# Three token blocks instead of two take turns over the first MLP's weights, with partial sums added up in DRAM

## The chip, the core and the metric

The kernel runs on one core of a Trainium2 chip. The metric is the device time of one execution in microseconds (us). The engines are PE (matrix products), DVE and ACT (vector and activation work, both read PSUM), POOL (vector work without PSUM), and SP, which in this kernel only issues DMAs.

## The reference, cut to what matters

```
X = fft(fft(x, axis=1), axis=2).real          # x: 2 x 3008 x 256
x = X.reshape(6016, 256)
h = x @ w_in;  g = relu(h) ** 2;  x = g @ w_out            # first MLP, 256 -> 2048 -> 256
h = x @ w2_in; g = h * sigmoid(1.702 * h); out = g @ w2_out # second MLP, the same sizes
```

## The kernel before

**Tiling.** The 6016 tokens (two batches) are eight blocks of some 752 columns, four blocks for each batch. A block's columns lie in two halves of 376 to 378 that share one product by symmetry. The kernel has an opening (loads of x, three folds of x and the transform along the features for batch 0, the first weights), then the first MLP for all blocks, and behind it the second MLP, which starts some 520 us into the span.

**Steps of the first MLP.** The hidden width of 2048 is cut into 16 chunks `f`, so there are 8 x 16 = 128 steps. Step i does in this order: `front1` (6 matmuls of chunk f into a psum tile of pool `psa`, 2 buffers), `back` of the step that lies four earlier (`LAG = 4`, 12 matmuls into the two accumulators of its block, pool `psb`, 2 buffers), then on DVE the row `p` (L685) and the two rows `h` (L687, L688), on ACT relu, square and the rounded part `gh` (L694, L695, L697; the steps in `SV` do relu and square on DVE, L692), and on POOL the remainder `gl` (L75; the steps in `VSTEPS` on DVE). A step is named below by its number, and it begins with its `p` on DVE.

**Weights.** They come as 64-bit words. `widen` makes of one group (4 chunks of f; there are 4 groups in, 4 groups out) an exact pair of a rounded part and a remainder: rows L158, L159, L166, L168 on DVE (L157, L163 on ACT; L165 on DVE in one case), L188 on POOL and L189 on DVE for the input weights, L191 on ACT, and the remainder on POOL (on DVE for in 1 and out 3). Group g of the input weights is needed when a step reaches f = 4g, group g of the output weights four steps later.

**Turns.** Because a group takes long to widen, the first two blocks take turns over what is there, and a block that leaves its turn unfinished writes its two accumulators to DRAM (`store`); `fetch_partial` reads them back and the block's last `store` adds them on DVE (L571):

```
turns = [(0, 0, 0, 4), (0, 1, 0, 8), (0, 0, 4, 16), (0, 1, 8, 16)]   # (mlp, block, from f, to f)
turns += [(0, j, 0, 16) for j in range(2, 8)]
```

**Background.** All other work (widening, the transform of further blocks, the folds of batch 1, the second MLP's weights) runs between the steps. `PLAN` gives for each job the step at which it begins, how many of its pieces are emitted for each step, and the step before which it must be through. `even_k` makes blocks 0 and 1 of a batch, `odd_k` blocks 2 and 3 (two sums of 16 matmuls of 376 columns each, L328, their evacuation L386 and L387, and `split_eo`, L336 and L75). The framework orders each engine's queue itself from the emitted program, and only from step 18 on (`THROTTLE`) background work is held behind the step's own rows. Every queue runs in order. `o` (the copy of an accumulator that is stored) and `h` share a ring of four buffers, so an `h` can wait until the DMA of an `o` has landed.

Of the kernel before, what the change touches and what calls it, by code (L numbers as in the profile page):

```python
# [16 lines left out]
P = 128  # L17
# [15 lines left out]
PLAN = {  # L33
# [29 lines left out]
def spectral_two_mlps_kernel(  # L63
# [33 lines left out]
    cp = tc.alloc_tile_pool(name="cp", bufs=3, side="right", reuse_waits="tile")  # L97
    xp = tc.alloc_tile_pool(name="xp", bufs=3, side="left")

# [3 lines left out]
    def load_x(q):  # L103
        b, c = divmod(q, NC)
        xq[q] = xp.tile([P, 2, 8, P], F32, tag="xt", name="xt")
        src = x8[b, c].rearrange("p (r a t) -> p r a t", r=2, a=8)
        for a in XPARTS[q]:
            nc.sync.dma_start(xq[q][:, :, a], src[:, :, a])
# [60 lines left out]

    def temp(pool):  # L170
        return pool.tile([P, 2, 1024], F32, tag="xt", name="ue")

    weights = {}

    def widen(mlp, kind, g, temps, dest, then=None):
        low = G if LOW[mlp, kind, g] == "G" else V
        raw = raws.pop((mlp, kind, g))
        ue = temp(temps)
        yield from narrow(raw, ue, (mlp, kind, g))
        if then:  # L180
# [73 lines left out]
    def fold(q, then=None):  # L254
# [3 lines left out]
        for a in XPARTS[q]:  # L258
            yield lambda: (
                G.tensor_tensor(out=t[:, 1, a], in0=xt[:, 0, a], in1=xt[:, 1, a], op=ALU.subtract),  # L260
                V.tensor_tensor(out=t[:, 0, a], in0=xt[:, 0, a], in1=xt[:, 1, a], op=ALU.add),
            )
# [23 lines left out]
        def part(par):  # L286
            ps = ps_a()
            cols = slice(0, 130) if par == 0 else slice(130, 258)
# [82 lines left out]

    def odd_k(b, pool):

        wd = WID[2]
        w = temp(pool).rearrange("p a b -> p (a b)")
        a = w[:, 0:wd]
# [22 lines left out]
        yield lambda: sums(1)  # L399
        yield lambda: split_eo(b, 2, e2)  # L400
        yield lambda: split_eo(b, 3, e3)
        yield lambda: nyquist(2)
        yield lambda: nyquist(3)
# [3 lines left out]

    turns = [(0, 0, 0, 4), (0, 1, 0, 8), (0, 0, 4, 16), (0, 1, 8, 16)]
    turns += [(0, j, 0, 16) for j in range(2, 8)]
    steps = [(mlp, j, f, f == lo, f == hi - 1) for mlp, j, lo, hi in turns for f in range(lo, hi)]  # L410
# [67 lines left out]
    def start():  # L478

        yield from fold(0, fold_nyquist)  # L480
        yield from fold(1)
        yield from fold(2)
        yield from both(widen(0, 0, 0, xp, winp, then=lambda: load_w(0, 0, 1)), small_w())
        yield from even_k(0, 0, h_temps)
        load_c(0, 3)
# [4 lines left out]
    run(start())  # L490

    def opening(g):
        nxt = g + 1 < 4
        jobs = [widen(0, 1, g, xp, wq, then=(lambda: load_w(0, 1, g + 1)) if nxt else None)]
        if nxt:
            jobs.append(widen(0, 0, g + 1, xp, winp,
                              then=(lambda: load_w(0, 0, g + 2)) if g + 2 < 4 else None))
        yield from both(*jobs)

# [9 lines left out]

    at("out0", lambda: widen(0, 1, 0, xp, wq, then=lambda: load_w(0, 1, 1)))  # L510
    at("in1", lambda: widen(0, 0, 1, xp, winp, then=lambda: load_w(0, 0, 2)))
    at("even01", lambda: even_k(0, 1, h_temps))
    at("out1", lambda: widen(0, 1, 1, xp, wq, then=lambda: load_w(0, 1, 2)))
    at("in2", lambda: widen(0, 0, 2, xp, winp, then=lambda: load_w(0, 0, 3)))
    at("out2", lambda: widen(0, 1, 2, xp, wq, then=lambda: load_w(0, 1, 3)))
    at("in3", lambda: widen(0, 0, 3, xp, winp))
    at("out3", lambda: widen(0, 1, 3, xp, wq))
    at("part0", lambda: iter([lambda: fetch_partial(0, xp)]))
    at("odd0", lambda: odd_k(0, xp))
    at("part1", lambda: iter([lambda: fetch_partial(1, xp)]))  # L520
    at("x3", lambda: iter([lambda: load_x(3)]))
# [30 lines left out]

    partial = {}

    def fetch_partial(j, pool):
        wd = WID[blocks[j][1]]
        t = temp(pool)
        t = t.rearrange("p a b -> p (a b)")[:, 0:4 * NP].rearrange("p (e s k) -> p e s k", e=2, s=2)
        nc.sync.dma_start(t[:, :, :, 0:wd], ydram[j][:, :, :, 0:wd])
        partial[j] = t[:, :, :, 0:wd]  # L560
# [103 lines left out]
    for i in range(n):  # L664
# [306 lines left out]
```

## Time and profile before

| what | value |
|---|---|
| median of 3 runs | 1035.78 us (1034.89 to 1036.43) |
| profiled execution, its own time | 1036.32 us |
| span of the profiled execution | 1034.5 us |
| PE busy over the span | 972.4 us (94%), 5496 matmuls |
| DVE busy | 822.5 us (80%) |
| ACT busy | 616.5 us (60%) |
| POOL busy | 351.3 us (34%) |
| DMA | 62.14 MB, q1 (issued by SP) alone carries the program's data |

The busy time of PE is modelled and pipelined, so a busy PE is not one at its peak. PE's granted clock is given as a share of 2.4 GHz; 0.5 is the lower level of 1.2 GHz. DVE rows that follow each other overlap by a little under 0.1 us.

### The profile page before, as it was taken

The page shows a single profiled execution, that of the slowest core. Times are in us where ns is not written, and L with a number is a line of the kernel's source. Part 1 is how long each engine was busy: PE and PEld are TensorE (multiplying, and loading weights), DVE is VectorE, ACT ScalarE, POOL GpSimd, SP SyncE. Part 2 cuts the span into 40 slices and gives each one's busy share as a digit, 9 for nine tenths or more (in the row PEclk, how much of TensorE's full clock was granted, in tenths as well). Part 3 has the DMA queues.
Part 4 walks back from the last instruction along what each step waited for, and adds up shares of the span by engine and source line. Part 5 has one row for each costly group of instructions (what it writes and reads, how often), then busy time and mean ns, then how long its engine had stood idle before and what let it go on. Part 6 is the DMA issues. An engine that isn't in the chain of part 4 may idle for free.

```text
span 1034.5 us, 14012 instructions
## 1 busy us (share of the span) xinstructions
PE 972.4 (94%) x5496; PEld 944.4 (91%) x5496; DVE 822.5 (80%) x1084; ACT 616.5 (60%) x760; POOL 351.3 (34%) x216
## 2 busy tenths in 40 slices
PE   3778799999998999999989999999999999999998
PEld 3568788998998898999989999999999999999997
DVE  6899969796877579777557978888887887988875
ACT  1476666565778587888845455454455545455443
POOL 4377833443667545976811200202020020200000
PEclk9899999899999999999999999999999999999999
DMA  7423314201133103111231001000010000100000
GB/s 285 145 79 127 112 41 146 71 1 33 61 112 112 72 32 122 53 49 56 87 109 64 30 31 31 30 1 31 31 30 31 27 26 9 30 31 1 30 1 30
DMA packets 20770, 62.14 MB, mean 60 GB/s; under 512 B 1760, under 2 KB 12128, under 8 KB 17504
## 3 DMA queue, kind: packets, MB, share of 16 engines
q1 hardware_dynamic: 20704, 61.24, 16.8%
q8 instruction: 43, 0.70, 0.3%
q14 instruction: 23, 0.19, 0.1%
HBM read 41.59 MB, written 19.65 MB: 59 GB/s over the span
## 4 chain that ended last, share of the span: by engine, by line
PE 49%; DVE 4%; ACT 3%; issue 1%; POOL 1%; DVEq 0%; ACTq 0%; POOLq 0%
PE psb L752 25%; PE psa L736 22%; PE psb L438 2%; ACT h L695 1%; ACT h L694 1%; DVE gl L75 0%; DVE ue L166 0%; DVE h L687 0%; DVE h L688 0%; DVE p L685 0%; ACT gh L697 0%; ACT ue L157 0%; DVE ue L158 0%; POOL gl L75 0%; POOL ue L599 0%
## 5 line engine op out<-in xcount | busy, mean ns | idle before, releaser
L75 POOL TENSOR_TENSOR gl<-h,gh 128x752 fp32r<-128x752 f32 (+1 forms) x113 | 223.5, 1988 | 166.9 <-ACT gh L697 137.5
L438 PE MATMUL psb<-gh,w 128*128 128x376 f32 (+1 forms) x1024 | 244.3, 341 | 7.9 <-ACT o L573 4.9
L752 PE MATMUL psb<-gh,w 128*128 128x376 f32 (+1 forms) x1024 | 237.7, 334 | 0.0
L438 PEld LDWEIGHTS psb<-gh,w 128*128 128x128 f32 x1024 | 186.3, 193 | 10.2 <-ACT o L573 6.3
L752 PEld LDWEIGHTS psb<-gh,w 128*128 128x128 f32 x1024 | 182.9, 188 | 0.0
L694 ACT ACTIVATE h<-h 128x752 f32<-128x752 f32 (+1 forms) x116 | 96.8, 834 | 75.4 <-DVE h L688 65.4
L438 PE MATMUL psb<-gl,w 128*128 128x376 f32 (+1 forms) x512 | 132.8, 341 | 2.5 <-POOL gl L75 2.5
L817 ACT ACTIVATE g<-c 128x1128 f32<-128x1128 f32 (+1 forms) x64 | 74.0, 1156 | 98.9 <-DVE c L815 98.9
L752 PE MATMUL psb<-gl,w 128*128 128x376 f32 (+1 forms) x512 | 129.9, 335 | 0.4 <-DVE gl L75 0.3
L599 POOL TENSOR_TENSOR ue<-raw 128x376 f32<-128x376 f32 (+1 forms) x16 | 14.9, 949 | 337.2 <-DVE ya L75 311.0
L697 ACT CAST gh<-h 128x752 fp32r<-128x752 f32 (+1 forms) x128 | 105.4, 825 | 27.8 <-DVE h L692 24.5
L685 DVE SCALAR_TENSOR_TENSOR p<-n,w1n_t,psa 128x376 f32<-128x376 f32 (+1 forms) x128 | 76.7, 600 | 46.9 <-PE psa L425 46.8
L75 DVE TENSOR_TENSOR gl<-g,gh 128x1504 fp32r<-128x1504 f32 (+1 forms) x64 | 111.4, 1741 | 2.7 <-ACT gh L797 1.6
L423 PE MATMUL psa<-eo,w 128*128 128x376 f32 (+1 forms) x256 | 90.0, 351 | 24.7 <-DVE h L688 19.0
L797 ACT CAST gh<-g 128x1504 fp32r<-128x1504 f32 (+1 forms) x64 | 93.1, 1455 | 29.3 <-DVE g L788 29.3
L695 ACT ACTIVATE h<-h 128x752 f32<-128x752 f32 (+1 forms) x116 | 97.1, 837 | 3.4
L438 PEld LDWEIGHTS psb<-gl,w 128*128 128x128 f32 x512 | 94.8, 193 | 3.3 <-POOL gl L75 3.2
L752 PEld LDWEIGHTS psb<-gl,w 128*128 128x128 f32 x512 | 92.1, 188 | 1.0 <-DVE gl L75 1.0
L814 DVE TENSOR_TENSOR g<-g,psa 128x376 f32<-128x376 f32 (+1 forms) x64 | 35.0, 547 | 70.9 <-ACT g L813 70.9
L788 DVE TENSOR_TENSOR g<-g,c 128x1128 f32<-128x1128 f32 (+1 forms) x64 | 89.0, 1390 | 1.2 <-ACT g L817 1.2
L424 PE MATMUL psa<-eo,w 128*128 128x376 f32 (+1 forms) x256 | 86.8, 339 | 0.0
L425 PE MATMUL psa<-eo,w 128*128 128x376 f32 (+1 forms) x256 | 86.8, 339 | 0.0
(130 smaller groups left out, 1600.4 us busy)
## 6 DMA issues: line engine op xcount, KB each, us to landing
ydram<-o SPq DMA_DIRECT2D x14, 376.0 KB, 3.4
xt<-in_x SPq DMA_DIRECT2D x5, 1024.0 KB, 5.0
cst<-in_dfts SPq DMA_DIRECT2D x8, 570.0 KB, 4.4
raw<-ydram SPq DMA_DIRECT2D x6, 752.0 KB, 4.8
out<-o SPq DMA_DIRECT2D x11, 376.0 KB, 3.1
raw<-in_w1i SPq DMA_DIRECT2D x4, 1024.0 KB, 5.3
raw<-in_w1o SPq DMA_DIRECT2D x4, 1024.0 KB, 5.8
raw<-in_w2i SPq DMA_DIRECT2D x4, 1024.0 KB, 4.9
```

The source lines that it names most:

```text
L75: eng.tensor_tensor(out=o, in0=a, in1=f32(b), op=ALU.subtract)
L423: T.matmul(o, lhsT=w[:, 0, fs], rhs=t[:, par, 0, 0:wd], start=True, stop=False)
L424: T.matmul(o, lhsT=w[:, 0, fs], rhs=t[:, par, 1, 0:wd], start=False, stop=False)
L425: T.matmul(o, lhsT=w[:, 1, fs], rhs=t[:, par, 0, 0:wd], start=False, stop=True)
L438: T.matmul(acc[j][ec][:, s, 0:wd], lhsT=w[:, hl, e0:e0 + P], rhs=(gh, gl)[gi][:, s, 0:wd], start=(first and hl == 0 and gi == 0), stop=(la ...
L694: A.activation(out=hv, in_=hv, func=AF.Relu)
L695: A.activation(out=hv, in_=hv, func=AF.Square)
L697: last_a = A.copy(gh[:, :, 0:wd], hv)
L736: T.matmul(bank, lhsT=w[:, hl, slot * P:(slot + 1) * P], rhs=t[:, yl, i], start=(first and hl == 0 and yl == 0), stop=(hl == 1), skip_grou ...
L752: T.matmul(o[:, s, 0:wd], lhsT=w[:, hl, e0:e0 + P], rhs=g[:, 2 * i + s, 0:wd], start=(f == 0 and hl == 0 and g is gh), stop=(f == 15 and h ...
L788: V.tensor_tensor(out=g[:, 1:4, 0:pw], in0=g[:, 1:4, 0:pw], in1=c[:, :, 0:pw], op=ALU.mult)
L797: A.copy(gh[:, :, 0:pw], g[:, :, 0:pw])
```

## The change

Three blocks take turns, in seven turns instead of four, before the remaining blocks follow. The widening of groups 1 to 3 becomes one chain (`conv`), alternately an input and an output group, from step 3 with 2 pieces a step, due by step 36. The transform of blocks 2 and 3 (`odd0`) moves from step 25 to step 1, since block 2 now begins at step 8; its last two pieces, which are for block 3, wait for step 36. Partial sums are no longer read back: the first `store` of a block writes, each later one is a DMA issued by POOL that adds to what lies in DRAM. The pool `xp` gets named places (`SPOT`), so that work buffers reuse particular folds' places; the two later folds of batch 0 do their subtraction on DVE in place of POOL; in batch 0 the second half of a fold's products uses `psb` in place of `psa`; the loads and folds of batch 1 get new places in `PLAN`.

```diff
 PLAN = {
-    "out0": (0, 12, 9), "in1": (0, 2, 8), "even01": (0, 1, 4), "out1": (4, 5, 12), "in2": (7, 5, 18),
-    "out2": (15, 3, 16), "in3": (12, 1, 16), "out3": (18, 1, 20), "part0": (13, 1, 20), "odd0": (25, 1, 32),
...
+    "out0": (0, 12, 3), "even01": (0, 1, 4), "odd0": (1, 1, 48), "conv": (3, 2, 36),
+    "x3": (14, 1, 20), "x4": (33, 1, 34), "fold3": (33, 2, 39), "fold4": (38, 2, 44), "fold5": (43, 2, 48),
...
+SPOT = ("x0", "x1", "x2", "x1", "x0", "x1")
...
-                G.tensor_tensor(out=t[:, 1, a], in0=xt[:, 0, a], in1=xt[:, 1, a], op=ALU.subtract),
+                (V if q in (1, 2) else G).tensor_tensor(out=t[:, 1, a], in0=xt[:, 0, a], in1=xt[:, 1, a], op=ALU.subtract),
...
-            ps = ps_a()
+            ps = ps_b() if b == 0 and par else ps_a()
...
+        yield lambda: nyquist(2)
+        while at_step[0] < later:
+            yield lambda: None
         yield lambda: split_eo(b, 3, e3)
-        yield lambda: nyquist(2)
...
-    turns = [(0, 0, 0, 4), (0, 1, 0, 8), (0, 0, 4, 16), (0, 1, 8, 16)]
-    turns += [(0, j, 0, 16) for j in range(2, 8)]
+    turns = [(0, 0, 0, 4), (0, 1, 0, 4), (0, 2, 0, 8), (0, 1, 4, 12), (0, 0, 4, 16), (0, 1, 12, 16), (0, 2, 8, 16)]
+    turns += [(0, j, 0, 16) for j in range(3, 8)]
...
+    at("conv", lambda: chain(*(
+        widen(0, k, g, xp, (winp, wq)[k], tag=("t", "x0")[k],
+              then=(lambda k=k, g=g: load_w(0, k, g + 1)) if g < 3 else None)
+        for g in (1, 2, 3) for k in range(2))))
...
-            if j in partial:
-                V.tensor_tensor(out=o[:, :, 0:wd], in0=partial[j][:, ec], in1=ap, op=ALU.add)
...
+            (A.copy, V.tensor_copy)[ec](o[:, :, 0:wd], ap)
+            if fresh:
+                nc.sync.dma_start(ydram[j][:, ec, :, 0:wd], o[:, :, 0:wd])
             else:
-                V.tensor_copy(o[:, :, 0:wd], ap)
-            nc.sync.dma_start(ydram[j][:, ec, :, 0:wd], o[:, :, 0:wd])
+                G.dma_start(out=ydram[j][:, ec, :, 0:wd], in_=o[:, :, 0:wd], accum_op=ALU.add)
```

What the queues become is shown at three places. First DVE in the opening, before: `t` is the work tile of a fold, `xt` its x (96, 103, 105 are folds 0, 1, 2), and L300 reads fold 0's products out of PSUM.

```order
L271 TENSOR_TENSOR xt_96<-xt_96 128x512
L261 TENSOR_TENSOR t_168<-xt_103 128x1024
L265 TENSOR_TENSOR xt_103<-t_168 128x512
L266 TENSOR_TENSOR xt_103<-t_168 128x512
L271 TENSOR_TENSOR xt_103<-xt_103 128x512
L261 TENSOR_TENSOR t_197<-xt_105 128x1024
L300 TENSOR_TENSOR zc_143<-psa_145,nyq_126 128x260 x2
L265 TENSOR_TENSOR xt_105<-t_197 128x512
```

The same place in the changed kernel (lines have moved; L260 is the subtraction, L301 the reading):

```order
L271 TENSOR_TENSOR xt_96<-xt_96 128x512
L260 TENSOR_TENSOR t_168<-xt_103 128x1024
L261 TENSOR_TENSOR t_168<-xt_103 128x1024
L265 TENSOR_TENSOR xt_103<-t_168 128x512
L266 TENSOR_TENSOR xt_103<-t_168 128x512
L271 TENSOR_TENSOR xt_103<-xt_103 128x512
L301 TENSOR_TENSOR zc_143<-psa_145,nyq_126 128x260 x2
L260 TENSOR_TENSOR t_197<-xt_105 128x1024
L261 TENSOR_TENSOR t_197<-xt_105 128x1024
```

DVE has two rows more, and the reading of fold 0's products stands ahead of fold 2's large rows instead of behind them.

Second DVE in step 1 before, from its rows `h` to the next step's `p` (`ue_431` is out 1 in the making, `w_394` in 1):

```order
L687 TENSOR_TENSOR h_331<-p_332,psa_324 128x378
L688 TENSOR_TENSOR h_331<-p_332,psa_324 128x378
L365 TENSOR_TENSOR n_351<-ht_349,psa_344 128x188
L366 TENSOR_TENSOR n_351<-ht_349,psa_344 128x188
L158 TENSOR_SCALAR ue_431<-ue_431 128x1024
L75 TENSOR_TENSOR w_394<-ue_304,w_394 128x1024
L685 SCALAR_TENSOR_TENSOR p_363<-n_270,w1n_t_125,psa_355 128x378
```

And in the changed kernel, from the same place on (`ue_593` is out 1, `ue_733` in 2, `ue_350` the first sum of blocks 2 and 3):

```order
L75 TENSOR_TENSOR w_519<-ue_413,w_519 128x1024
L159 TENSOR_SCALAR ue_593<-ue_593 128x1024
L166 SCALAR_TENSOR_TENSOR ue_593<-raw_299,ue_593 128x1024
L168 ISA ue_593<-ue_593 128x2048
L158 TENSOR_SCALAR ue_733<-ue_733 128x1024
L166 SCALAR_TENSOR_TENSOR ue_733<-raw_517,ue_733 128x1024
L388 TENSOR_TENSOR ue_350<-ue_350,psa_351 128x376
L389 TENSOR_TENSOR ue_350<-ue_350,psa_351 128x376
L668 SCALAR_TENSOR_TENSOR p_371<-n_270,w1n_t_125,psa_363 128x378
```

Rows of two weight groups and of the transform stand ahead of step 2's `p`, where before step 2 followed at once. The queue of steps 4 to 17, on the other hand, holds after the change no widening row at all; out 2, in 3 and out 3 are finished in steps 18 to 31.

Third POOL where block 1's second turn ends (step 27), in the changed kernel, with the semaphores each row waits for (DMAHW1 and DMAHW2 are the earlier writes of the same place in DRAM):

```order
L75 TENSOR_TENSOR w_1134<-ue_1037,w_1134 128x1024 [waits Activation_49]
L260 TENSOR_TENSOR t_1434<-xt_799 128x1024 [waits DMAHW6_49,Pool_49]
L558 DMA ydram_683<-o_1225 128x2x376 [waits DMAHW1_49,Activation_49]
L558 DMA ydram_683<-o_1228 128x2x376 [waits DMAHW2_49,DVE_49]
L75 TENSOR_TENSOR gl_1269<-h_1220,gh_1233 128x756 [waits PE_49,Activation_49]
```

Two DMAs stand in POOL's queue there, where before POOL had none. On DVE the row that takes the first one's `o` buffer again is this one, in step 29, seven rows behind the copy that made `o_1228`:

```order
L554 COPY o_1228<-psb_978 128x2x376 [waits Pool_49]
L668 SCALAR_TENSOR_TENSOR p_1293<-n_270,w1n_t_125,psa_1273 128x378 [waits DVE_49,PE_49]
L75 TENSOR_TENSOR gl_1235<-h_1187,gh_1194 128x756 [waits Activation_49]
L158 TENSOR_SCALAR ue_1198<-ue_1198 128x1024 [waits Activation_49]
L670 TENSOR_TENSOR h_1260<-p_1261,psa_1239 128x378 [waits DVE_49]
L159 TENSOR_SCALAR ue_1198<-ue_1198 128x1024 [waits DVE_49]
L671 TENSOR_TENSOR h_1260<-p_1261,psa_1239 128x378
L670 TENSOR_TENSOR h_1292<-p_1293,psa_1273 128x378 [waits DMASW0_49]
```

`DMASW0` is the adding DMA of `o_1225`. There are four such ends of a turn, with two adding DMAs each (steps 27, 39, 43 and 51).

## Rows read from the trace of the kernel before

**Rows 1.** Stages: length, busy us (instructions) by engine, PE clock, DMA share, GB/s

```profile
0.00:46.67 46.67, 25.33 (x140) 22.69 (x140) 33.69 (x47) 12.15 (x17) 17.92 (x17) 0.85 0.59 218
46.67:66.08 19.41, 13.63 (x73) 11.47 (x73) 19.41 (x27) 14.20 (x18) 11.65 (x7) 1.00 0.21 78
66.08:115.06 48.98, 42.13 (x224) 39.90 (x225) 48.91 (x61) 36.86 (x45) 36.68 (x19) 0.97 0.41 134
115.06:237.29 122.23, 113.41 (x619) 106.97 (x618) 101.80 (x144) 76.96 (x96) 57.28 (x31) 0.94 0.19 64
```

**Rows 2.** DVE in order of time (start, us): `p` of steps 0, 5, 18, 48

```profile
46.67 0.61 DVE L685 SCALAR_TENSOR_TENSOR p<-n,w1n_t,psa 128x378 f32<-128x378 f32 x1 [1.73 <-PE psa L425]
...
66.08 0.60 DVE L685 SCALAR_TENSOR_TENSOR p<-n,w1n_t,psa 128x376 f32<-128x376 f32 x1
...
115.06 0.59 DVE L685 SCALAR_TENSOR_TENSOR p<-n,w1n_t,psa 128x378 f32<-128x378 f32 x1
...
237.29 0.61 DVE L685 SCALAR_TENSOR_TENSOR p<-n,w1n_t,psa 128x376 f32<-128x376 f32 x1 [2.28 <-PE psa L425]
```

**Rows 3.** PE: first matmul of two neighbouring steps; then one sum of blocks 2, 3

```profile
118.75 0.33 PE L423 MATMUL psa<-eo,w 128*128 128x378 f32 x1
...
121.87 0.34 PE L423 MATMUL psa<-eo,w 128*128 128x378 f32 x1
...
143.92 4.15 PE L328 MATMUL psa<-cst,zc 128*128 128x376 f32 x16
```

**Rows 4.** Opening, DVE in order of time

```profile
18.40 3.37 DVE L261 TENSOR_TENSOR t<-xt 128x1024 f32<-128x1024 f32 x1
21.69 0.75 DVE L300 TENSOR_TENSOR zc<-psa,nyq 128x260 f32<-128x260 f32 x2
...
36.38 3.40 DVE L166 SCALAR_TENSOR_TENSOR ue<-raw,ue 128x1024 uint32<-128x1024 uint32 x1
39.70 0.54 DVE L354 TENSOR_TENSOR ht<-ht,psa 128x378 f32<-128x378 f32 x1
```

**Rows 5.** Opening, POOL, PE and ACT in order of time

```profile
17.89 2.80 POOL L260 TENSOR_TENSOR t<-xt 128x1024 f32<-128x1024 f32 x1 [2.62 <-DVE xt L266]
...
22.54 10.17 PE L292 MATMUL psa<-dft,xt 128*128 128x130 f32 x64 [3.21 <-issue]
...
41.60 0.68 PE L423 MATMUL psa<-eo,w 128*128 128x378 f32 x1 [5.01 <-ACT eo L336]
...
35.23 1.05 ACT L191 CAST w<-ue 128x1024 fp32r<-128x1024 f32 x1 [1.89 <-DVE ue L189]
40.73 0.82 ACT L336 CAST eo<-ht 128x756 fp32r<-128x756 f32 x1 [3.77 <-DVE ht L355]
```

**Rows 6.** DVE at step 30: the same large row with POOL not beside it

```profile
169.52 1.22 DVE L261 TENSOR_TENSOR t<-xt 128x1024 f32<-128x1024 f32 x1
```

**Rows 7.** DVE groups from 20 to 260: busy us, mean ns, then idle before

```profile
L166 DVE SCALAR_TENSOR_TENSOR ue<-raw,ue 128x1024 uint32<-128x1024 uint32 x8 | 17.3, 2168 | 0.0
L168 DVE CUSTOM_DVE_ANT_0 ue<-ue 128x2048 uint16<-128x2048 uint16 x8 | 11.5, 1444 | 0.0
L159 DVE TENSOR_SCALAR ue<-ue 128x1024 uint32<-128x1024 uint32 x8 | 9.3, 1158 | 0.0
L158 DVE TENSOR_SCALAR ue<-ue 128x1024 f32<-128x1024 f32 x8 | 8.6, 1070 | 0.0
L189 DVE SCALAR_TENSOR_TENSOR ue<-ue,mask 128x512 f32<-128x512 f32 x4 | 5.1, 1281 | 0.0
L75 DVE TENSOR_TENSOR eo<-ue,eo 128x752 fp32r<-128x752 f32 x2 | 3.0, 1482 | 0.1
L386 DVE TENSOR_TENSOR ue<-ue,psa 128x376 f32<-128x376 f32 x2 | 1.1, 545 | 3.7 <-ACT ue L385 3.7
```

**Rows 8.** DMA issues: KB each, median us from issue to landing

```profile
ydram<-o SPq DMA_DIRECT2D x14, 376.0 KB, 3.4
...
raw<-ydram SPq DMA_DIRECT2D x6, 752.0 KB, 4.8
```

More of the change, by code (lines that the diff above doesn't have):

```diff
@@ L97, in spectral_two_mlps_kernel @@
     cp = tc.alloc_tile_pool(name="cp", bufs=3, side="right", reuse_waits="tile")
-    xp = tc.alloc_tile_pool(name="xp", bufs=3, side="left")
+    xp = tc.alloc_tile_pool(name="xp", bufs=1, side="left")
     xq = {}
@@ L104, in load_x @@
         b, c = divmod(q, NC)
-        xq[q] = xp.tile([P, 2, 8, P], F32, tag="xt", name="xt")
+        xq[q] = xp.tile([P, 2, 8, P], F32, tag=SPOT[q], name="xt")
         src = x8[b, c].rearrange("p (r a t) -> p r a t", r=2, a=8)
@@ L168, in narrow, with temp, widen @@
         yield lambda: V.tensor_tensor(out=uu, in0=uu, in1=eu, op=ALU.add)
-    def temp(pool):
-        return pool.tile([P, 2, 1024], F32, tag="xt", name="ue")
+    def temp(pool, tag="xt"):
+        return pool.tile([P, 2, 1024], F32, tag=tag, name="ue")
     weights = {}
-    def widen(mlp, kind, g, temps, dest, then=None):
+    def widen(mlp, kind, g, temps, dest, then=None, tag="xt"):
         low = G if LOW[mlp, kind, g] == "G" else V
         raw = raws.pop((mlp, kind, g))
-        ue = temp(temps)
+        ue = temp(temps, tag)
         yield from narrow(raw, ue, (mlp, kind, g))
@@ L318, in spectral_two_mlps_kernel @@
     eo, e128 = {}, {}
+    at_step = [0]
     def halves(even, odd, terms, fresh=True):
@@ L370, in even_k, with odd_k @@
         yield nyquist
-    def odd_k(b, pool):
+    def odd_k(b, pool, tag="xt", later=0):
         wd = WID[2]
-        w = temp(pool).rearrange("p a b -> p (a b)")
+        w = temp(pool, tag).rearrange("p a b -> p (a b)")
         a = w[:, 0:wd]
@@ L482, in start @@
         yield from fold(2)
-        yield from both(widen(0, 0, 0, xp, winp, then=lambda: load_w(0, 0, 1)), small_w())
+        yield from both(widen(0, 0, 0, wq, winp, tag="w", then=lambda: load_w(0, 0, 1)), small_w())
         yield from even_k(0, 0, h_temps)
@@ L490, in spectral_two_mlps_kernel @@
     run(start())
[L492 to L498, printed above, removed]
     plan = {}
@@ L508, in at @@
             due.setdefault(end, []).append(name)
-    at("out0", lambda: widen(0, 1, 0, xp, wq, then=lambda: load_w(0, 1, 1)))
-    at("in1", lambda: widen(0, 0, 1, xp, winp, then=lambda: load_w(0, 0, 2)))
+    at("out0", lambda: widen(0, 1, 0, xp, wq, tag="x0", then=lambda: load_w(0, 1, 1)))
     at("even01", lambda: even_k(0, 1, h_temps))
[L513 to L520, printed above, removed]
+    at("odd0", lambda: odd_k(0, xp, "x2", 36))
+    at("conv", lambda: chain(*(
+        widen(0, k, g, xp, (winp, wq)[k], tag=("t", "x0")[k],
+              then=(lambda k=k, g=g: load_w(0, k, g + 1)) if g < 3 else None)
+        for g in (1, 2, 3) for k in range(2))))
     at("x3", lambda: iter([lambda: load_x(3)]))
@@ L551, in background @@
             assert name in gone, name
[L553 to L560, printed above, removed]
     def store(j, f):
         wd = WID[blocks[j][1]]
-        if f == 15 or j not in partial:
-            ydram[j] = dram.tile([P, 2, 2, NP], F32, tag=f"y{j}_{f}", name="ydram")
+        fresh = j not in ydram
+        if fresh:
+            ydram[j] = dram.tile([P, 2, 2, NP], F32, tag=f"y{j}", name="ydram")
         for ec in range(2):
@@ L569, in store @@
             ap = acc[j][ec][:, :, 0:wd]
-            if j in partial:
-                V.tensor_tensor(out=o[:, :, 0:wd], in0=partial[j][:, ec], in1=ap, op=ALU.add)
-            elif ec == 0:
-                A.copy(o[:, :, 0:wd], ap)
-            else:
-                V.tensor_copy(o[:, :, 0:wd], ap)
-            nc.sync.dma_start(ydram[j][:, ec, :, 0:wd], o[:, :, 0:wd])
+            (A.copy, V.tensor_copy)[ec](o[:, :, 0:wd], ap)
+            if fresh:
+                nc.sync.dma_start(ydram[j][:, ec, :, 0:wd], o[:, :, 0:wd])
+            else:
+                G.dma_start(out=ydram[j][:, ec, :, 0:wd], in_=o[:, :, 0:wd], accum_op=ALU.add)
     pend = None
@@ L675, in spectral_two_mlps_kernel @@
             w2b = tc.alloc_tile_pool(name="w2b", bufs=3, side="left", reuse_waits="tile")
+        at_step[0] = i
         j, f = steps[i][1:3]
```

3 rows, old and new, of the table PLAN are left out of this document.

## The prediction

> **What bounds the kernel now.** I read the stages first, since shares over the whole span mix them. The boundaries are the starts of the steps 0, 5, 18 and 48 [rows 2]. In the opening no engine is full. From step 0 to step 17 DVE is: 19.41 of 19.41 us and 48.91 of 48.98 us [rows 1], while PE, which could go on every 3.12 us (121.87 - 118.75) [rows 3], takes 68.4 us for 18 steps, 3.8 us each. From step 18 to step 47 neither is full: 122.23 us for 30 steps, with DVE idle for 20.4 us (122.23 - 101.80) [rows 1]. Behind step 48 the change leaves all rows in place except the last two adding DMAs, in step 51.
>
> So before step 48 there are three things to gain: the opening, the 0.7 us a step in which DVE is late, and the 20.4 us in which DVE is idle. DVE's total work is hardly changed: the same eight groups are widened, the same folds made, and an add of a partial sum (L571) is exchanged for a copy of the same size (L575). The question is whether DVE's idle time shrinks, and what PE does meanwhile.
>
> **The change part by part. The opening.** Fold 1 and fold 2 have their subtraction on POOL, and DVE's own large row beside it takes 3.37 us, POOL's 2.80 us [rows 4, 5]; the same DVE row at step 30 takes 1.22 us [rows 6]. Two of them in sequence on DVE cost some 2.3 us (they overlap a little), so each fold is about 1.0 us shorter though DVE does more. The reading of fold 0's products (L300) starts at 21.69 us because it stands behind fold 2's large row [rows 4]; in the new order it stands ahead, at 17.4 us (18.40 - 1.0). That, and `psb` for the second half, lets PE start fold 1 directly behind fold 0 instead of at 22.54 us [rows 5]. PE then waits for fold 2's data, at 24.4 us as now, and if its clock falls again to the lower level, fold 2's products end some 1.2 us earlier than now. DVE's L166 at 36.38 us, which takes 3.40 us beside POOL and holds up L354 behind it [rows 4], now comes before POOL's row. What is late next is ACT: the cast L191, which took 1.05 us from 35.23 us, stands ahead of the copy that L354 needs. I get the rounded `eo` at 38.6 us instead of 41.55 us (40.73 + 0.82 [rows 5]), and the first `p` at 43.3 us instead of 46.67 us [rows 2]: **-3.4 us**. Ends: -1.2 us if only PE's chain counts, -6.0 us if PE keeps the upper clock and ACT's cast gets out of the way.
>
> **Steps 0 to 4.** Their DVE rows grow by: L168 of out 1 (1.44 us), all five rows of in 2 (1.07 + 1.16 + 2.17 + 1.44 + 1.28), L158 of out 2 (1.07), four evacuations of the sums (4 x 0.55) and one `eo` (1.48) [rows 7]: 13.3 us, or 12.3 us since rows overlap a little. This stage is full now, so it becomes 31.7 us instead of 19.4 us. The two sums (4.15 us each [rows 3]) lie on PE under this and cost nothing as long as DVE is the later one; if the wait lets PE's clock fall they take twice that, and up to 4 us would show.
>
> **Steps 5 to 17.** These lose their widening: 21.5 us by the same rows, 20.3 us with overlap, so DVE has 28.6 us of work where it had 48.9 us [rows 1]. Now PE sets the pace: 13 x 3.12 = 40.6 us, and 0.4 us for one turn's end more than now, 41.0 us instead of 49.0 us. DVE is idle here for over 12 us.
>
> **Steps 18 to 47.** They take over the rest of out 2 (4.8 us) and in 3 (7.1 us) and give up the sums' four rows and one `eo` (3.7 us): 101.8 + 8.2 - 0.4 = 109.6 us of DVE, against 30 x 3.12 = 93.6 us and some 6 us of folds on PE. DVE is the later one. Of the 20.4 us idle now, 8.3 us are PE's two sums, which are gone; of the rest I keep 7.0 us, since the folds of batch 1 still make PE and DVE wait for each other: 116.6 us instead of 122.2 us. Ends: 3 us and 12 us of idle time, 112.6 and 121.6 us.
>
> From step 0 to step 48 that is 31.7 + 41.0 + 116.6 = 189.3 us instead of 190.6 us: **-1.3 us**. The work was spread by the plan's numbers, but up to step 18 nothing holds a background row back, so the widening of out 1 and in 2 was pulled into steps 1 and 2, and idle time only moved from the thirties to steps 5 to 17.
>
> **The adding DMAs.** No DMA of POOL and none that adds is in the trace. They hold an `o` buffer until they have landed, and the `h` behind it waits, as L670 `h_1292` does for DMASW0. Between copy and that `h` lie seven rows or less, by [rows 1, 7] some 4.4 us at step 27, and by the same count 6.6, 8.0 and 6.4 us at steps 39, 43 and 51. What the DMA takes is bounded by the plain write of the same size, 3.4 us, and by that plus the reading back of both accumulators, 3.4 + 4.8 = 8.2 us [rows 8]. I take the write plus half the read, since one DMA carries half: 5.8 us. Then 1.4 us show at step 27 and none elsewhere: **+1.4 us**. At 3.4 us nothing shows, at 8.2 us 3.8 + 1.6 + 0.2 + 1.8 = 7.4 us. The time for which POOL is busy with issuing is unknown too; a `gl` behind it is needed only four steps later, so a few us are hidden.
>
> Here a page gives a price of its own. The Trainium skill, DMA: Bandwidth & Descriptors, section "Anatomy of one DMA — SWDGE (gpsimd) path", fits a DMA issued by GpSimd at 2.0 us plus its bytes at 436 GB/s. For 376 KB that is an estimate of 2.9 us, below even the plain write's 3.4 us in the trace; by it the term is 0 and the sum 1.4 us lower. No run here shows such a DMA, and the page does not say that the fit covers an adding one, so I stay with the rows.
>
> **Sum.** -3.4 - 1.3 + 1.4 = -3.3 us. Against the profiled execution's 1036.3 us this is 1033.0 us; the median of the runs is 0.5 us lower than that execution, so I forecast **1032.5 us**.
>
> **The rivals.** A measurement of this kernel can tell about 0.2%, 2.1 us, from no change; that bound is meant below.
>
> *More is gained.* If DVE, with more work than PE over 30 steps, hardly ever idles in steps 18 to 47 (3 us, -4.0), and the opening gains 6.0 us (-2.6), the time is near 1026. For it: in steps 0 to 17 now DVE does not idle at all [rows 1]. Against it: PE and DVE wait for each other wherever folds are made, and they still are.
>
> *Nothing is left.* The lump in steps 1 and 2 lets PE run dry, its clock is lower when the sums come, and 3 us show there; or only 1.2 us come from the opening. Either puts the time at 1034.5 to 1036. For it: PE's clock is 0.85 in the opening and 0.94 in steps 18 to 47, so it does fall when PE waits [rows 1]. Against it: in steps 0 to 4 DVE is behind in any case.
>
> *It gets slower by the adding DMAs.* The place is the `h` in steps 29, 41, 45 and 53; it decides from about 8.1 us of landing time on, where 1.4 us grow to 7.0 us (3.7 + 1.5 + 0.1 + 1.7). At 10 us the four stalls are 5.6 + 3.4 + 2.0 + 3.6 = 14.6 us and the time is 1045.7 us. For it: POOL has `t` of fold 3 ahead of the first pair, a row of 2.80 us [rows 5], and an adding DMA reads as well as writes. Against it: the plain write lands in 3.4 us [rows 8], and step 27 alone is tight. The Trainium skill, SBUF — State Buffer, section "SBUF: two separate sides", speaks for this rival: POOL cannot write such a DMA's descriptors while DVE holds the shared port pair; no run here shows it yet. As a mechanism of this kernel: L158 and L159 of out 3 stand on DVE just behind the copies, and if POOL's issue waits for both (1.07 + 1.16 us [rows 7]), 5.8 us become 8.0 us and the time is 1037.7 us (3.6 + 1.4 + 1.6 = 6.6 us instead of 1.4).
>
> *It gets slower by idle time.* If the 12 us of idle time in steps 18 to 47 stay and 3 us show in the lump, the time is 1032.5 + 5.0 + 3.0 = 1040.5 us.
>
> **Chances.** The forecast case 0.37, around 1032.5 (1030 to 1033.7); more gained 0.13; nothing left 0.26; slower by the DMAs 0.13; slower by idle time 0.11. So faster 0.50, same 0.26, slower 0.24. The range for 8 in 10 reaches from 1026 to 1041: it leaves out the DMA case beyond some 9 us of landing and the end of the gain.
>
> **What would show it.** Right: the first `p` near 43 us; `p` of step 5 near 75 us, later than now; steps 5 to 17 at 3.1 us each with DVE some 60 to 70% busy; step 18 within 2 us of now's 115 us; step 48 near 234 us; adding DMAs that land in 5 to 7 us. Wrong: a first `p` later than 45 us; steps 5 to 17 slower than 3.4 us each, because POOL's `gl` or the two more ends of turns hold PE; idle time of DVE over 12 us behind step 18; an `h` that waits for a DMA by more than 3 us in several steps; or a difference that arises behind step 53, where the sum has none.

## The result and the profile after

The changed kernel takes 1042.63 us (median of 4 runs, 1042.13 to 1043.40); the kernel before, run beside it on the same chip, 1035.51 us. The ratio is 1.0069, 95% interval 1.0051 to 1.0086: it is 0.7% slower, where 0.3% faster was forecast. The profiled execution spans 1041.6 us against 1034.5 us.

The stages of the changed kernel, by windows (length, then busy time of PE, weight loads, DVE, ACT and POOL with the count of instructions, granted clock, DMA share, GB/s); they answer to [rows 1], and the boundaries are again the first `p` of the steps 0, 5, 18 and 48:

```profile
0.00:40.16 40.16, 22.71 (x142) 19.97 (x142) 30.71 (x49) 12.08 (x17) 14.59 (x15) 0.92 0.72 277
40.16:75.75 35.59, 28.87 (x114) 21.53 (x111) 31.82 (x41) 20.39 (x26) 17.38 (x9) 0.81 0.40 138
75.75:113.69 37.94, 37.68 (x217) 36.82 (x215) 28.25 (x45) 28.80 (x37) 24.82 (x14) 1.00 0.11 42
113.69:243.97 130.28, 109.47 (x591) 104.58 (x591) 108.59 (x148) 80.43 (x101) 65.21 (x38) 0.93 0.26 65
```

Up to step 18 the change is 1.4 us ahead of [rows 2]; the loss comes later. Steps 18 to 47 take 130.28 us instead of 122.23 us (129.46, 129.35 and 129.70 us in three other executions whose rows in these steps are the same, e0_after, e4_odd1 and e7_noopen below), and DVE is idle there for 21.7 us (130.28 - 108.59), no less than the 20.4 us before. Step 48 begins 6.7 us late. By step 90 the lag is 10.1 us (402.99 against 392.86 us), and the end is 7.1 us late. The waits of steps 18 to 47 (total, times, longest) say who waits for whom:

```profile
DVE p L668 <- PE psa L429: 13.7, 10, 4.4
PE psa L427 <- DVE h L671: 8.7, 5, 4.3
PE psa L293 <- DVE xt L277: 8.1, 3, 3.4
DVE zc L301 <- PE psa L293: 5.3, 2, 2.8
```

PE and DVE wait for each other, above all where a fold is made: L293 is a fold's product, which waits for the fold's last rows on DVE, and the steps behind it on PE wait with it. Before, such waits at L292 were 3.2 us in all. The adding DMAs landed as forecast, in the profile's list of DMA issues (last number: median us to landing):

```profile
ydram<-o POOLq DMA_DIRECT2D x6, 376.0 KB, 5.8
...
ydram<-o POOLq DMA_DIRECT2D x2, 378.0 KB, 6.2
```

Yet something happens beside them. The timeline of the changed kernel at step 29 and step 40 (start, duration):

```profile
152.28 2.40 POOL L260 TENSOR_TENSOR t<-xt 128x1024 f32<-128x1024 f32 x1
154.63 2.57 POOL L558 DMA_DIRECT2D ydram<-o  x2
155.41 4.16 DVE L158 TENSOR_SCALAR ue<-ue 128x1024 f32<-128x1024 f32 x1
156.27 2.74 POOL L75 TENSOR_TENSOR gl<-h,gh 128x756 fp32r<-128x756 f32 x1
159.50 0.54 DVE L670 TENSOR_TENSOR h<-p,psa 128x378 f32<-128x378 f32 x1
...
206.94 1.79 POOL L558 DMA_DIRECT2D ydram<-o  x2
207.99 5.48 DVE L271 TENSOR_TENSOR xt<-xt 128x512 f32<-128x512 f32 x1
208.12 3.03 POOL L260 TENSOR_TENSOR t<-xt 128x1024 f32<-128x1024 f32 x1
210.46 2.46 POOL L75 TENSOR_TENSOR gl<-h,gh 128x752 fp32r<-128x752 f32 x1
213.40 0.53 DVE L670 TENSOR_TENSOR h<-p,psa 128x376 f32<-128x376 f32 x1
...
233.38 0.68 DVE L271 TENSOR_TENSOR xt<-xt 128x512 f32<-128x512 f32 x1
```

L271 takes 0.68 us alone (at 233.38 us) and 5.48 us at step 40, where it ends only when POOL is through with its issues, `t` and `gl`, which stand one behind the other. The `h` behind it is late by as much, and PE with it.

### The profile page after: what moved, and what is told of

Its sections match the earlier page's. It is cut to its first block, busy times and chain, and to the rows that moved or that the text cites. A ratio compares the mean times of both kernels' runs of the same rounds, so it can differ in the third digit from the quotient of the medians.

```text
span 1041.6 us, 14019 instructions
## 1 busy us (share of the span) xinstructions
PE 975.5 (94%) x5496; PEld 945.5 (91%) x5496; DVE 819.3 (79%) x1086; ACT 618.2 (59%) x764; POOL 351.3 (34%) x222
## 4 chain that ended last, share of the span: by engine, by line
PE 49%; DVE 2%; POOL 1%; ACT 1%; issue 0%; DVEq 0%; ACTq 0%; POOLq 0%
PE psb L735 25%; PE psa L719 22%; PE psb L442 1%; DVE gl L75 0%; POOL gl L75 0%; POOL ue L581 0%; DVE yc L75 0%; POOL w L75 0%; DVE ue L166 0%; ACT h L677 0%; ACT h L678 0%; PE psa L429 0%; PE psa L428 0%; ACT gh L680 0%; PE psa L427 0%
## 5 line engine op out<-in xcount | busy, mean ns | idle before, releaser
L75 POOL TENSOR_TENSOR gl<-h,gh 128x752 fp32r<-128x752 f32 (+1 forms) x113 | 220.5, 1959 | 170.9 <-ACT gh L680 125.6
L427 PE MATMUL psa<-eo,w 128*128 128x376 f32 (+1 forms) x256 | 90.7, 354 | 23.2 <-DVE h L671 15.1
L428 PE MATMUL psa<-eo,w 128*128 128x376 f32 (+1 forms) x256 | 88.1, 344 | 0.0
L429 PE MATMUL psa<-eo,w 128*128 128x376 f32 (+1 forms) x256 | 87.6, 342 | 0.0
```

Source lines behind the costliest of these rows:

```text
L75: eng.tensor_tensor(out=o, in0=a, in1=f32(b), op=ALU.subtract)
L427: T.matmul(o, lhsT=w[:, 0, fs], rhs=t[:, par, 0, 0:wd], start=True, stop=False)
L428: T.matmul(o, lhsT=w[:, 0, fs], rhs=t[:, par, 1, 0:wd], start=False, stop=False)
L429: T.matmul(o, lhsT=w[:, 1, fs], rhs=t[:, par, 0, 0:wd], start=False, stop=True)
```

## The experiments

Theory: the loss behind step 18 has two causes, folds packed into a few steps and adding DMAs that cost more than their landing; a third loss comes from the odd sums of batch 1. Rivals: the lump of widening in steps 1 and 2, or one cause alone. Each ratio is against runs of the kernel before on the same chip.

**The opening alone (e1_opening).**

```
 kernel before:
-    G.tensor_tensor(out=t[:, 1, a], ...)
+    (V if q in (1, 2) else G).tensor_tensor(out=t[:, 1, a], ...)
-            ps = ps_a()
+            ps = ps_b() if b == 0 and par else ps_a()
```

> The kernel before, with the two edits of the opening alone (folds 1 and 2 subtract on DVE, the second half of a fold's products goes to psb); turns, plan and the adding by DVE stay. Theory: the opening is worth what the first p of the changed kernel showed (40.16 us against 46.67 us) and, since DVE has no idle time in steps 0 to 17 of the kernel before, nothing there can swallow it: first p at 40 to 41 us, step 18 near 109 us, time 1029 to 1031 us. Rival: the lead is given back at the first wait that doesn't depend on DVE (a load, or PE's two sums in steps 25 and 26): first p at 40 to 41 us, but step 48 back at 236 to 237 us and the time 1034 to 1036 us.

Measured: 1033.60 us, ratio 0.9994 (0.9980 to 1.0008). The first `p` is at 41.41 us, 5.3 us early, step 3 at 56.43 us, only 1.7 us early, step 48 at 235.59 us. The rival is nearer: the lead is not kept. But it was lost in steps 0 to 2 and not at the load or the sums that the rival named: PE waited there for POOL's `gl` of step 1, 2.8 us, and its granted clock in steps 0 to 4 was 0.78 (1.00 before).

**Plain writes for the adding ones (e2_plain).**

```
-    G.dma_start(out=ydram[j][:, ec, :, 0:wd], in_=o[:, :, 0:wd], accum_op=ALU.add)
+    part = dram.tile([P, 2, NP], F32, ...)
+    nc.sync.dma_start(part[:, :, 0:wd], o[:, :, 0:wd])
```

> The changed kernel, with each adding DMA replaced by SP's plain write of the same tile to a place of its own, so that the partial sums of the blocks 0 to 2 are left out of the output; DVE's rows stand in the same order. Theory that POOL's issues are dear (their rows of 1.8 to 2.6 us, and DVE's L158 of 4.16 us in step 29 and L271 of 5.48 us in step 40 beside them): step 29 falls from 14.3 us to 9 or 10 us, step 40 from 7.4 us to 4 or 5 us, and the time to 1035 to 1038 us. Rival, that the loss behind step 18 is one of placement (three folds and three widenings packed into steps 18 to 47, with DVE idle 21.7 us where 7.0 us were forecast): the rows of 4 to 5 us stay, since POOL's tensor rows stretch them, steps 18 to 47 stay at 127 to 130 us and the time at 1040 to 1043 us.

Measured: 1036.66 us, ratio 1.0018 (1.0007 to 1.0029). Steps 18 to 47 by windows:

```profile
113.83:236.98 123.15, 108.47 (x591) 103.56 (x591) 103.98 (x147) 80.65 (x101) 59.57 (x32) 0.94 0.19 68
```

So the six adding DMAs of this stage (the last two come behind it, at 263.42 us) cost 7.1 us (130.28 - 123.15), or 6.2 us against the 129.35 us of e4_odd1; by the two ratios it is 0.0051 or 5.3 us. It arises where the DMAs stand: step 29 takes 12.04 us instead of 14.34 us (9 to 10 were expected), step 40 5.30 instead of 7.44 us, step 44 3.37 instead of 4.95 us. The timeline of this run at step 40 shows how:

```profile
204.76 2.39 POOL L260 TENSOR_TENSOR t<-xt 128x1024 f32<-128x1024 f32 x1 [0.68 <-POOL gl L75]
205.06 2.63 DVE L271 TENSOR_TENSOR xt<-xt 128x512 f32<-128x512 f32 x1
207.10 2.27 POOL L75 TENSOR_TENSOR gl<-h,gh 128x752 fp32r<-128x752 f32 x1
207.62 0.53 DVE L671 TENSOR_TENSOR h<-p,psa 128x376 f32<-128x376 f32 x1
```

Without the issues `t` stands earlier, L271 waits it out alone and takes 2.63 us instead of 5.48 us. But 19.2 us of DVE's idle time are left (123.15 - 103.98), so this is not the whole loss.

**POOL issues plain writes (e8_poolplain).**

```
+    G.dma_start(out=part[:, :, 0:wd], in_=o[:, :, 0:wd])
```

> The changed kernel, with POOL issuing plain writes to places of their own in place of the adding ones (the partial sums of the blocks 0 to 2 are left out of the output): the issue on POOL stays, the adding goes. Theory: the 6 to 7 us that the adding DMAs cost in steps 18 to 47 come from POOL's issue rows, which push its t and gl rows together so that a DVE row started beside them lasts until POOL is through: L158 of step 29 stays near 4.2 us, L271 of step 40 near 5.5 us, steps 18 to 47 stay at 128 to 131 us, the time at 1041 to 1043 us. Rival: the adding holds the o buffers longer (5.8 us from issue to landing) and an h waits for it: the plain write lands in 3 to 4 us, steps 18 to 47 take 123 to 125 us as with SP's writes, the time is 1036 to 1038 us.

Measured: 1039.69 us, ratio 1.0035 (1.0020 to 1.0051); steps 18 to 47 take 126.16 us, L158 of step 29 3.10 us, L271 of step 40 4.80 us. Neither theory holds alone: POOL's issuing costs 3.0 us (126.16 - 123.15), the adding the other 4.1 us, or 3.2 us against e4_odd1. All issues of this run on POOL, with duration (min/median/max, ns) and landing (us):

```profile
L559 POOL DMA_DIRECT2D part<-o x8: 562/684/803, 155.5 to 261.4; - x8
...
DMA to landing us min/median/max: 2.7/3.3/4.1
```

and those of the changed kernel:

```profile
L558 POOL DMA_DIRECT2D ydram<-o x8: 902/1205/1693, 154.6 to 264.7; - x8
...
DMA to landing us min/median/max: 4.9/5.8/7.4
```

An adding DMA holds POOL nearly twice as long as a plain one, and lands 2.5 us later.

**Adding DMAs in the kernel before (e6_addb).** `store` as in the changed kernel; turns and plan stay, the readings back go.

> The kernel before, its turns and plan kept, with the sums of blocks 0 and 1 added by POOL's adding DMAs (four of them, at the ends of steps 27 and 35) in place of the two readings back by SP and DVE's four adds (two of which become copies by DVE, two by ACT). Theory that an adding DMA costs by what stands beside it on POOL: 1 to 2 us a pair, as in the changed kernel (7.1 us for four pairs), so 1.5 to 4 us, 1036 to 1038.5 us on this chip. Rival: with DVE's adds and the readings gone as well, the exchange is even and the time within 1 us of the kernel before.

Measured: 1038.11 us, ratio 1.0026 (1.0011 to 1.0041): 2.7 us for two pairs, within what the theory said. Where it arises is less clear: in the one profiled execution steps 18 to 47, where the DMAs stand, are 1.2 us longer (123.48 us), and steps 69 to 72, where no row was changed, 2.7 us (12.53 us instead of 9.79 us). Those four steps take 12.59 us in e0_after and 9.78 us in e7_noopen, whose rows there are the same, so that part need not come from the DMAs.

**Fold subtractions on DVE (e10_foldv).**

```
-    (V if q in (1, 2) else G).tensor_tensor(out=t[:, 1, a], ...)
+    (V if q else G).tensor_tensor(out=t[:, 1, a], ...)
```

> The changed kernel, with the subtraction of the folds 3, 4 and 5 on DVE too: POOL gives up three rows of 2.4 to 3.1 us, DVE takes on three of 1.22 us. Theory that DVE's rows are stretched by POOL's tensor rows beside them: DVE's L75 of step 29 (3.08 us), L271 of steps 34 and 40 (2.89 and 5.48 us) and L266 of step 44 (3.00 us) fall to 0.7 to 1.4 us each, 3.7 us come back on, and steps 18 to 47 are 4 to 6 us shorter: 1036.5 to 1038.5 us. Rival: other rows of POOL (gl, the DMA issues) take the place of t and DVE has more to do: 1042 to 1045 us.

Measured: 1039.35 us, ratio 1.0037 (1.0021 to 1.0054); steps 18 to 47 take 125.18 us, DVE is busy for 102.89 us although it has 3.7 us more to do. Step 29 in its timeline:

```profile
156.90 0.55 DVE L670 TENSOR_TENSOR h<-p,psa 128x378 f32<-128x378 f32 x1 [4.17 <-DMA ydram<-o]
157.37 0.69 DVE L158 TENSOR_SCALAR ue<-ue 128x1024 f32<-128x1024 f32 x1
```

L158 is back at 0.69 us, and now the wait of `h` for the landing is seen, 4.17 us, which L158 had covered (in this run `h` also stands ahead of L158 in DVE's queue). Both prices of the adding DMA are real; they lie over each other. The stage is 5.1 us shorter, as the theory said, but the time falls by 0.0032 or 3.3 us alone, to just above the theory's range.

**Folds spread (e5_folds).**

```
-    "fold3": (33, 2, 39), "fold4": (38, 2, 44), "fold5": (43, 2, 48),
+    "fold3": (28, 1, 38), "fold4": (34, 1, 45), "fold5": (39, 1, 48),
```

> The changed kernel, with the folds 3, 4 and 5 begun in steps 28, 34 and 39 and made one part a step in place of two a step from 33, 38 and 43. Theory that the idle time behind step 18 comes from the packing: PE, in order, waits at the fold's products (L293) for xt 8.1 us, DVE after it for p; with the parts spread those waits fall below 4 us, DVE idles 12 to 16 us in place of 21.7 us, and the time is 1036 to 1039 us. Rival: the stalls move along with the rows, since each fold still has POOL's t beside DVE's rows and PE behind both: steps 18 to 47 stay at 127 us or more, 1040 to 1044 us.

Measured: 1034.64 us, ratio 0.9999 (0.9984 to 1.0014). Steps 18 to 47:

```profile
114.41:236.38 121.97, 106.21 (x587) 100.62 (x587) 106.39 (x147) 81.22 (x101) 66.37 (x38) 0.96 0.28 69
```

8.3 us less (130.28 - 121.97); PE's wait for `xt` at L293 is gone, DVE idles 15.6 us.

**Folds spread and plain writes (e13_foldplain).**

> The changed kernel with the folds spread, and SP's plain writes to places of their own in place of the adding DMAs (the partial sums of the blocks 0 to 2 are left out of the output). Theory that what the adding DMAs cost is their collision with the packed folds on POOL: with the folds spread they cost little, steps 18 to 47 take 119 to 122 us beside 122.0 us with the adding ones, the time is 1032 to 1034.5 us. Rival: they have a price of their own, 5 to 7 us wherever the folds are: steps 18 to 47 take 115 to 117 us, 1027.5 to 1030 us.

Measured: 1031.59 us, ratio 0.9954 (0.9941 to 0.9968). Steps 18 to 47:

```profile
114.78:232.89 118.11, 105.58 (x587) 100.34 (x587) 104.52 (x148) 81.32 (x101) 60.58 (x32) 0.97 0.20 71
```

The four runs make a square: 130.28 and 123.15 us with packed folds (adding, plain), 121.97 and 118.11 us with spread ones. Adding costs 7.1 us (6.2 us against e4_odd1) beside packed folds and 3.9 us beside spread ones, between the theory and its rival: by the stages part is collision with the folds, part its own. The ratios do not separate the two (0.0051 and 0.0045, each ratio uncertain by 0.001 or more). The edit of the folds also lets them begin 4 to 5 steps earlier, so the square does not tell the packing from the place.

**The odd sums in the old order (e4_odd1).**

```
 yield lambda: split_eo(b, 2, e2)
-yield lambda: nyquist(2)
+if later:
+    yield lambda: nyquist(2)
...
 yield lambda: split_eo(b, 3, e3)
+if not later:
+    yield lambda: nyquist(2)
```

> The changed kernel, with the order inside the odd sums of batch 1 (steps 79 to 88) put back as in the kernel before: both splits of eo, then both Nyquist products. Theory: PE's wait for eo at L395 (1.8 us behind POOL, 0.7 us behind DVE in the changed kernel, none in the one before) is where the lag grows from 7.4 us at step 82 to 10.2 us at step 86: the time falls by 2.5 to 3 us, to 1039.5 to 1040.5 us. Rival: those steps lose by what comes late from ahead of them (PE has no idle time there to make up for it), and the time stays within 1 us of the changed kernel's 1042.6 us.

Measured: 1041.08 us, ratio 1.0065 (1.0045 to 1.0085), between what the theory and the rival said, and by itself not to be told from 1.0069. The trace tells more: steps 72 to 89 take 66.76 us, 66.79 us before and 69.50 us in the changed kernel, where PE's waits in these steps were

```profile
PE psa L395 <- POOL eo L75: 1.8, 1, 1.8
...
PE psa L395 <- DVE eo L75: 0.7, 1, 0.7
```

The edit of `odd_k`, made for batch 0, also moved batch 1's first Nyquist product ahead of the second split, so that PE reaches it before `eo` is ready: 2.7 us in these steps.

**Both repairs (e11_both).**

> The changed kernel with both repairs: folds 3 to 5 one part a step from 28, 34 and 39, and the odd sums of batch 1 in the order of the kernel before. Theory that the two losses are separate and add up (8.3 us in steps 18 to 47, of which the first repair showed 1034.6 us; 2.75 us in steps 72 to 90): 1031 to 1033 us, 0.2 to 0.4% below the kernel before. Rival: the second is made up elsewhere, since the same repair alone moved the median by only 1.5 us: 1033.5 to 1035.5 us.

Measured: 1032.84 us, ratio 0.9974 (0.9961 to 0.9986), 0.0025 or 2.6 us below the folds alone: the losses add up, and this version beats both kernels. The changed kernel itself on that chip (e0_after):

> The changed kernel itself, so that the times beside it come from one chip: 1041 to 1043 us, 0.6 to 0.8% over the kernel before; its stages within 1 us of the first profile's behind step 18 (130.3 us for steps 18 to 47), since neither theory lets them vary more.

Measured: 1044.31 us, ratio 1.0075 (1.0062 to 1.0088), steps 18 to 47 129.46 us.

**Both repairs and fold subtractions on DVE (e12_bothv).**

> As the run before, and the subtraction of the folds 3 to 5 on DVE too. Theory that POOL's t rows stretch the DVE rows beside them in the spread folds as well (DVE's rows of 29 to 46 that take 1.7 to 4.2 us where the same form alone takes 0.4 to 1.2 us fall): another 2 to 3 us less, 1029 to 1031 us. Rival: with the folds spread, DVE is the fuller engine in steps 29 to 46 and its three rows more (3.7 us) use up what the stretching gives back: 1031 to 1034 us.

Measured: 1036.80 us, ratio 1.0005 (0.9994 to 1.0016), a miss: steps 18 to 47 take 125.19 us. What helps packed folds by about 3 us harms spread ones by about 3 us. The rival's reason, that DVE is the fuller engine there, is not shown: against the run with both repairs DVE is busy for 0.7 us more (107.14 against 106.44 us) but idle for 2.6 us more (18.05 against 15.49 us). Why stays open.

**The lump held back (e3_thr3).** `THROTTLE = 18` becomes `THROTTLE = 3`.

> The changed kernel with THROTTLE = 3 in place of 18: the background rows are held back behind their step from step 3 on, so that the rows of in 1, out 1 and in 2 stand in steps 4 to 16 in place of steps 1 and 2. Theory that the lump in steps 1 and 2 costs time of its own: steps 0 to 4 take 22 to 25 us in place of 35.6 us, steps 5 to 17 take 41 to 45 us in place of 37.9 us, step 18 begins 4 to 7 us earlier and the time is 1036 to 1039 us. Rival: the DVE work only moves, step 18 begins within 2 us of 113.7 us and the time is 1041 to 1043 us.

Measured: 1048.83 us, ratio 1.0138 (1.0116 to 1.0159). By windows, the steps 0 to 4, 5 to 17 and 18 to 47:

```profile
42.54:66.34 23.80, 21.61 (x108) 16.27 (x109) 14.66 (x27) 13.71 (x20) 8.87 (x5) 1.00 0.21 75
66.34:115.17 48.83, 42.32 (x222) 40.81 (x221) 42.86 (x59) 35.97 (x44) 29.48 (x15) 0.93 0.27 97
115.17:250.46 135.29, 112.88 (x592) 108.59 (x591) 112.97 (x149) 81.97 (x104) 67.95 (x40) 0.91 0.24 62
```

The theory falls. Steps 0 to 17 take 72.6 us, and with the lump 73.5 us in the first profile and 71.6 us in e0_after: what the lump costs in steps 0 to 4, steps 5 to 17 give back at PE's pace. And steps 18 to 47 lose 5.0 us more. With both repairs (e16_thrfold):

> The changed kernel with both repairs and THROTTLE = 3. Theory that holding the widening back is bad by itself, as the longer time of THROTTLE = 3 alone says (1.0138 of the kernel before, against 1.0069 for the changed kernel): DVE idles in steps 0 to 4 and is full later; 1.003 to 1.005 of the kernel before. Rival: that loss came from the packed folds behind step 18, into which the held-back rows ran; with the folds spread the time is within 0.2% of the two repairs alone (0.9974).

Measured: 1034.12 us, ratio 0.9993 (0.9981 to 1.0006), steps 18 to 47 124.88 us: against both repairs alone (0.9974, 121.93 us) 2.0 us of the time and 3.0 us of the stage stay, where beside packed folds 7.1 us of the time (1.0138 - 1.0069) and 5.0 us of the stage were lost. So the packed folds made up part of the loss; the cause of the rest is open.

**The changed kernel without the opening (e7_noopen).**

> The changed kernel without the two edits of the opening. Theory: the opening's lead is swallowed in steps 0 to 2, as in the kernel before with those edits alone (5.3 us at the first p, 1.7 us at step 3): first p at 45 to 47 us, step 5 1 to 3 us later than with them, time 1043 to 1046 us, 0.8 to 1.0% over the kernel before. Rival: the changed kernel's fuller steps 0 to 4 keep the lead, since DVE has work ahead of PE there: step 5 is 4 to 6 us later and the time 1047 to 1050 us.

Measured: 1050.11 us, ratio 1.0142 (1.0121 to 1.0163); first `p` at 45.09 us, step 5 at 80.23 us, step 18 at 119.70 us, against 41.76, 75.07 and 113.39 us in e0_after. Here the opening is worth 3.3 us at the first `p`, 5.2 us at step 5, 6.3 us at step 18 (119.70 - 113.39) and 0.7% of the time. The rival is right that the lead is not swallowed; its reason, that DVE has work ahead of PE there, would keep a lead and not enlarge it, and is not shown.

**Block 1's `eo` on DVE, before with the opening (e14_openv) and repaired (e15_bestv).** In `LOWE`, `(0, 1): "G"` becomes `"V"`.

> The kernel before with the opening's two edits and block 1's second half of eo on DVE (0.94 us) in place of POOL (2.11 us, at 46.94 us with those edits alone, ahead of the gl for which PE waited 2.8 us). Theory: POOL's chain is what swallows the lead: step 3 at 54 to 55.5 us in place of 56.43 us, step 18 at 111 to 112.5 us, time 1.5 to 2.5 us below that of the opening's edits alone (0.9975 to 0.9985 of the kernel before). Rival: DVE, full up to step 17, pays for the row: step 18 stays at 113 to 114 us, the ratio at 0.999 to 1.000.

> The changed kernel with both repairs (folds spread, odd sums in the old order) and block 1's second half of eo on DVE. Theory: POOL's chain sets steps 1 to 3 here too: step 5 1 to 2 us earlier, 0.995 to 0.9965 of the kernel before. Rival: steps 0 to 4 are full of DVE's widening, which the row only lengthens: 0.997 to 0.998, as with the two repairs alone.

Measured: 1034.79 us, 0.9996 (0.9982 to 1.0010), and 1031.43 us, 0.9972 (0.9958 to 0.9986). In the first, step 3 comes at 52.69 us, 3.7 us earlier than with the opening alone, so POOL's chain did swallow the lead; but step 18 is at 113.91 us again (113.44 us with the opening alone): it is lost anew between steps 12 and 18, where DVE is nearly full. Both rivals hold on the time.

## Why the prediction was wrong

**What bounds the kernel** was read rightly up to step 18, and one sentence on the rest was wrong: that behind step 48 all rows but two DMAs stay in place. The reordered odd sums stand there, at 2.7 us.

**The opening** was forecast at -3.4 us with the first `p` at 43.3 us. It came at 40.16 and 41.76 us in two executions, and at 39.88 to 42.94 us in all profiled executions with both edits; without them it came at 45.09 to 46.67 us. The edits are worth some 7 us in the changed kernel (1.0142 against 1.0075) and less than the measurement can tell in the old one. The forecast lies between; what it lacked is that the worth of a lead depends on the next stage.

**Steps 0 to 4** took 35.59 us, 31.7 us forecast. DVE's work was right (31.82 us); the rest is the upper end named there, PE at a granted clock of 0.81, with the first odd sum taking 6.68 us instead of 4.15 us. About half of this belongs to the execution: e0_after takes 33.31 us at 0.90, and its first odd sum 5.17 us. **Steps 5 to 17** took 37.94 us, 41.0 us forecast: PE-bound as said, with DVE 74% busy (28.25 of 37.94), but at 2.92 us a step (37.94 / 13); the 3.12 us that the forecast read from one pair of steps was too long. That the two errors nearly cancel is luck.

**Steps 18 to 47 are the step that failed**: "of the rest I keep 7.0 us", for 116.6 us. DVE's idle time did not shrink: 21.7 us, and 19.2 us without the adding DMAs. The 8.3 us that were to come from PE's two sums do not show in it. In their place stand the plan's new numbers for the folds: folds 4 and 5 are now made two parts a step, as fold 3 was before, and all three begin later (DVE's rows of fold 4 lie in steps 38 to 41, before in 35 to 41), and PE, in order, waits for them. That these numbers cost the time is shown by e5 and e13: with the folds one part a step and begun earlier, the stage takes 118.11 us without the adding, 5.0 us less than packed, with DVE idle for 13.6 us, and is close to the forecast. Whether it is the rate or the later begin was not separated. The forecast had seen that idle time only moves, for steps 5 to 17, but took the folds as unchanged. It had named idle time of DVE over 12 us as a sign of being wrong.

**The adding DMAs** were the second: +1.4 us forecast, 6.2 to 7.1 us measured in this stage (3.9 us beside spread folds). Their landing, 5.8 us, was forecast to the tenth; the price was sought in the wrong place. In step 29 DVE's `o` copy ends at 150.80 us, but POOL has `w` and `t` ahead and issues at 154.63 us, 3.8 us later, which the sum left out and only a rival named. And the issue pushes `t` and `gl` together, so that a DVE row beside them takes 4 to 5 us.

The misses close the sum: -3.1 (opening), +3.9 (steps 0 to 4), -3.1 (steps 5 to 17), +12.3 (steps 18 to 47 with the adding: 130.28 - 116.6 - 1.4) and +0.4 us (behind step 48) are 10.4 us, from -3.3 us forecast to +7.1 us by the spans. The two rivals that forecast a loss, by the adding DMAs and by idle time, came true together; but the first had priced the landing, which was to decide from about 8.1 us on, and it was 5.8 us. Behind step 48 two things nearly cancel, the odd sums and the end: from step 127 to the last instruction 515.24 us instead of 518.23 us, with the granted clock at 1.00 instead of 0.88 in the first 14 us. Another execution of the changed kernel has 0.88 there and takes 516.86 us, so a part belongs to the execution and not to the change; the rest stays open.

## What to carry to other kernels

A job that is begun later and made in fewer steps can cost the in-order engine behind it even if the total work stays the same: where a plan's numbers change, look at the begin, at the rate per step and at who waits for the job's last row, before crediting freed idle time. A DMA that is issued by a computing engine is priced by what stands ahead of it and behind it in that engine's queue, not by its landing alone. An edit inside a shared helper changes every caller, so each caller's rows have to be compared.

## What the runs showed of the hardware

DVE's L271, whose inputs are both in SBUF, lasts longer beside POOL's rows: 0.68 us alone, 2.63 us beside `t`, 5.48 us where two issues, `t` and `gl` follow each other. An `h` (L671), which also reads PSUM, took 0.53 us beside `gl`. The Trainium skill, SBUF — State Buffer, section "SBUF: two separate sides", calls the port pair that the two engines share an exclusive lock held for a whole instruction, where the one that starts first blocks the other. The trace agrees that they exclude each other: L271 ends at 207.69 us in e2, 0.54 us behind the end of `t` (207.15 us), and at 213.47 us in the changed kernel, 0.55 us behind the end of `gl` (212.92 us). Who started first does not settle it in the rows: in the changed kernel L271 starts at 207.99 us, before `t` at 208.12 us, and still ends after both of POOL's rows. In e2 it ends ahead of `gl`, although `gl` follows `t` without a gap there too. Why DVE gets in between in one case and not in the other is not shown.

A plain DMA of 376 KB issued by POOL landed after 3.3 us, an adding one after 5.8 us, with 0.68 and 1.2 us of POOL's time for each. The Trainium skill, DMA: Bandwidth & Descriptors, section "Anatomy of one DMA — SWDGE (gpsimd) path", by whose fit the prediction estimated 2.9 us, is near the plain one; the adding one takes twice that, and for it the section gives no figure of its own.
